# Sparse attention and ELU layer on one core: the weights queue up behind the second block's Q, block three loads on GpSimd's queue, the first batch goes in three blocks

## The chip, the core and the metric

The kernel runs on one core of one Trainium2 chip. A core has five engines that run side by side, each through its own instructions in their written order: TensorE (PE, matrix products into PSUM; PEld is its loading of the stationary operand), VectorE (DVE), ScalarE (ACT), GpSimd (POOL) and SyncE (SP, which here only issues transfers). Transfers are issued by SP, ACT or POOL and carried by 16 shared DMA engines; the profile counts those that SP and ACT issue as queues of the kind hardware_dynamic, those that POOL issues as software_dynamic. An instruction that waits holds up everything written behind it on its engine. The metric is device time in microseconds (us).

## What is computed

Four batches of eight heads, 768 positions, 64 numbers a head. Each query takes part only in its six best chunks of 32 keys, found by a bound from each chunk's smallest and largest key; then an ELU layer of two matrix products follows.

```
k_min, k_max = min, max of k over each chunk of 32          # [B, H, 24, D]
ub = sum(maximum(q * k_min, q * k_max), axis=-1)            # [B, H, S, 24], causal
top_chunks = argsort(ub)[..., -6:]
scores = where(chunk selected and causal, q @ k.T / 8, -1e9)
x = softmax(scores) @ v                                     # to [3072, 512]
h = x @ w_in                                                # [3072, 2048]
out = where(h > 0, h, exp(min(h, 0)) - 1) @ w_out           # [3072, 512]
```

## The kernel before, in words

The work is cut into eight blocks: each batch in two halves of 384 queries (BLOCKS, line 40). A block goes through these stages; heads are handled in four pairs.

- **Loads** (`load`, L347 on). K, Q and V in f32, rows of 256 bytes. The first block's are fetched head by head (L365, 96 KB each), those of all others in tiles of 128 positions (L372, 256 KB each). SP issues nearly all of them; ACT issues four K loads of the first block. POOL issues the weights, w_in in four parts (L382) and w_out in four (L387); they are cast to bf16 on the way, and POOL issues them where the order puts them: w_in behind the first block's Q casts (G_IN), w_out behind the second's (G_OUT).
- **Front** (`prep_k`, `prep_q`). PE turns each K and Q tile (L401, 3 products with the identity for a pair). DVE reduces K to chunk minima and maxima (L420, L437). ACT copies K to bf16: in the first block straight into `lhs` (L427), in others into `kb` (L432), which SP then sends to `lhs` (L435). ACT copies Q in f32 (L452); POOL casts it to bf16 in `rhs` (L461); DVE makes its positive part (L464).
- **Selection** (`select`). PE makes the bounds (L481), DVE turns them (L492), finds the sixth best (L499), compares (L503) and turns the mask (L508); SP sends it in eight transfers into rows 64 to 95 of `rhs` (L512). The same rows of `lhs` hold a constant pattern (econst), put there by DVE (L336), ACT (L338) and SP (L341), so that the score product itself adds -40000 to what is not selected.
- **Attention** (`attend`). Score products (L533), exponentials on ACT (L549, L553), the causal diagonal on DVE (L560, L567), products with V (L581; V is cast by POOL, L392), normalising on DVE (L590, L592), then the turn to the layer's layout, by PE in the first and last block (L600) and by a transposing transfer in the others (L605).
- **Layer** (`mlp`). First product (L618), exponential on ACT (L622), subtraction on POOL (L624), maximum and minimum on DVE (L626), second product (L636), copy on ACT (L640), output by SP (L643).

No loop on the chip sets the order. All steps are noted in a list, each with an engine, a supposed duration, its dependences and a due time, shifted by the table SHIFTS; `Plan.run` plays them against numbered buffers (CAPS) and the resulting order is written out, engine by engine. On the chip each engine then waits for what its next instruction needs, in that order.

Of the kernel before, what the change touches and what calls it, by code (L numbers as in the profile page):

```python
# [15 lines left out]
B = 4  # L16
# [11 lines left out]
HS = S // 2  # L28
HCH = NCH // 2
# [7 lines left out]
Q0 = TOPK * CHUNK  # L37
QLO = (Q0, HS)
QHI = (HS, S)
BLOCKS = [(b, hf) for b in range(B) for hf in range(2)]  # L40
DIRECT_K = (0, )
DIRECT_Q = ()
INIT = ("DVE", "DVE", "ACT", "ACT")
G_IN = "q0"
G_OUT = "q1"
BY_PAIR = (0, )
AFTER_MASK = 1
GATED = ()
# [67 lines left out]
class Plan:  # L116
# [38 lines left out]
    def run(self):  # L155
# [7 lines left out]
        slots = {c: [(0.0, i, None) for i in range(n)] for c, n in self.caps.items()}  # L163
        free = dict.fromkeys(("PE", "ACT", "DVE", "POOL", "SP"), 0.0)
        cand = {e: [] for e in free}
        for o in self.ops:
            if o.wait == 0:
                cand[o.eng].append(o)
        best, dirty, held = dict.fromkeys(free), set(free), set()
        hw, sw, self.order = 0.0, 0.0, []  # L170
        for o in self.ops:
            for x in o.bufs:
                x.end = 0
        while len(self.order) < len(self.ops):
            for e in dirty:
                best[e], found = None, []
                for o in cand[e]:
                    t = max(o.ready, free[e])
                    for x in o.bufs:
                        if x not in held:  # L180
                            t = max(t, min(slots[x.cls], key=lambda v: v[:2], default=(1e18, ))[0])
# [51 lines left out]
def kernel(  # L233
# [448 lines left out]
    for s in range(NPAIR):  # L682
        init_lhs(s, INIT[s])
# [73 lines left out]
```

## Time and profile before

| what | value |
|---|---|
| median of 3 runs | 326.98 us (323.62 to 327.88) |
| the profiled execution | 325.89 us, its span 324.10 us |
| PE busy | 274.39 us, 85% of the span |
| ACT, DVE, POOL busy | 193.86, 190.84, 126.26 us |
| moved by DMA over the span | 36.49 MB, 113 GB/s in the mean |
| chain that ended last | PE 57%, DMA 15%, SP's queue 11%, ACT 7% |

The span runs from the profile's first instruction to its last; 1.79 us of the execution lie outside it. A busy share over the whole span mixes a start, in which data is still coming in, with a long middle in which PE is busy almost without a break; so the stretches are read apart below. The granted clock is given as a share of full speed (1.00 is 2.4 GHz, 0.50 is 1.2 GHz).

### The profile page before, as it was taken

What the parts mean: (1) busy time and instruction counts of PE and PEld (TensorE: products, weight loads), DVE (VectorE), ACT (ScalarE), POOL (GpSimd) and SP (SyncE); (2) the same over time, 40 slices, a digit from 0 to 9 for tenths busy, and PEclk for the clock granted to TensorE, in tenths of its full rate; (3) what the DMA queues carried; (4) which work ended last, traced back from release to release, by engine and by line L of the source; (5) the groups of instructions that cost most, each with busy time, mean ns of one, the idle gap of its engine ahead of it and who ended that gap; (6) DMA issues with size and microseconds to landing.
All of it is one profiled execution on the core that took longest, in us unless ns stands there. A gap on an engine that the chain in (4) does not pass through costs nothing.

```text
span 324.1 us, 6738 instructions
## 1 busy us (share of the span) xinstructions
PE 274.4 (85%) x2300; PEld 165.1 (51%) x2328; DVE 190.8 (59%) x603; ACT 193.9 (60%) x416; POOL 126.3 (39%) x251
## 2 busy tenths in 40 slices
PE   4722870797992999799989999999999999999995
PEld 2411540464662664366646654566665645664642
DVE  7540884383871698236875986689746823651730
ACT  6512730386882674399837743798888925871731
POOL 5550193284522154235553532256415403510730
PEclk9965897699998699999999999999999999999999
DMA  8899799689967379632904692311112021002101
GB/s 168 197 203 200 161 163 199 138 166 214 205 113 170 72 166 208 134 112 55 188 16 123 130 212 81 124 33 31 38 27 72 20 63 67 2 2 91 41 32 65
DMA packets 100690, 36.49 MB, mean 113 GB/s; under 512 B 88624, under 2 KB 97584, under 8 KB 100656
## 3 DMA queue, kind: packets, MB, share of 16 engines
q1 hardware_dynamic: 94832, 31.48, 44.8%
q0 software_dynamic: 4224, 4.19, 7.9%
q10 hardware_dynamic: 1600, 0.39, 0.6%
q8 instruction: 18, 0.29, 0.4%
q14 instruction: 16, 0.13, 0.1%
HBM read 27.26 MB, written 6.29 MB: 104 GB/s over the span
## 4 chain that ended last, share of the span: by engine, by line
PE 57%; DMA 15%; SPq 11%; ACT 7%; DVE 4%; issue 4%; POOL 2%; ACTq 0%; DVEq 0%; POOLq 0%
PE psM L618 19%; PE psM L636 19%; PE psS L533 8%; DMA kld<-in_k_dram 6%; DMA rhs<-msk 5%; PE psO L581 4%; SPq L372 4%; PE psT L401 4%; ACT pt L549 3%; SPq L512 3%; SPq L365 2%; ACT e L622 2%; DMA qld<-in_q_dram 2%; POOL e L624 1%; PE psT L481 1%
## 5 line engine op out<-in xcount | busy, mean ns | idle before, releaser
L624 POOL TENSOR_SCALAR e<-e 128x384 f32<-128x384 f32 x128 | 65.9, 518 | 114.2 <-ACT e L622 105.2
L618 PE MATMUL psM<-xt,w_in_sb 128*128 128x384 bf16 x512 | 103.1, 330 | 0.4
L636 PE MATMUL psM<-w_out_sb,gT 128*128 128x512 bf16 x356 | 98.0, 381 | 2.9 <-DVE gT L626 1.6
L626 DVE SCALAR_TENSOR_TENSOR gT<-psM,e 128x384 bf16<-128x384 f32 x128 | 69.6, 553 | 40.5 <-POOL e L624 38.1
L549 ACT ACTIVATE pt<-psS 128x384 bf16<-128x384 f32 (+1 forms) x156 | 79.2, 545 | 20.5 <-PE psS L533 19.4
L622 ACT ACTIVATE e<-psM 128x384 f32<-128x384 f32 x128 | 64.0, 504 | 35.5 <-PE psM L618 34.1
L533 PE MATMUL psS<-rhs,lhs 96*128 96x384 bf16 (+2 forms) x280 | 65.2, 301 | 11.2 <-DMA rhs<-msk 10.7
L618 PEld LDWEIGHTS <-w_in_sb 128*128 128x128 bf16 x512 | 49.3, 99 | 32.8 <-issue 4.2
L636 PEld LDWEIGHTS <-gT 128*128 128x128 bf16 x384 | 36.8, 98 | 33.8 <-DVE gT L626 2.9
L461 POOL TENSOR_SCALAR rhs<-QTf 64x384 bf16<-64x384 f32 x64 | 34.4, 538 | 44.6 <-ACT QTf L452 33.3
L533 PEld LDWEIGHTS <-lhs 96*128 96x128 bf16 x288 | 27.1, 102 | 30.2 <-DMA rhs<-msk 12.4
L640 ACT ACTIVATE osb<-psM 128x512 f32<-128x512 f32 x24 | 14.1, 597 | 36.0 <-PE psM L636 35.5
L420 DVE TENSOR_REDUCE kmx<-psT 128x12 f32<-128x384 f32 x28 | 15.5, 553 | 32.9 <-PE psT L401 32.8
L401 PE MATMUL psT<-ident_f,kld 128*128 128x128 f32 x84 | 16.9, 306 | 20.6 <-DMA kld<-in_k_dram 13.2
L581 PEld LDWEIGHTS <-pt 128*128 128x128 bf16 x672 | 28.8, 99 | 8.4 <-issue 0.8
L581 PE MATMUL psO<-vext,pt 128*128 128x65 bf16 x672 | 31.9, 196 | 0.1
L392 POOL TENSOR_SCALAR vext<-vld 128x384 bf16<-128x384 f32 x32 | 15.8, 518 | 24.8 <-DMA vld<-in_v_dram 17.7
L432 ACT ACTIVATE kb<-psT 128x384 bf16<-128x384 f32 x28 | 13.9, 497 | 18.7 <-DVE kst L420 12.7
L560 DVE TENSOR_TENSOR pt<-pt,tri 128x512 bf16<-128x512 bf16 x32 | 14.4, 449 | 17.0 <-ACT pt L549 16.8
L401 PEld LDWEIGHTS psT<-ident_f,kld 128*128 128x128 f32 x84 | 10.7, 153 | 26.5 <-DMA kld<-in_k_dram 14.7
L452 ACT ACTIVATE QTf<-psT 128x384 f32<-128x384 f32 x28 | 14.1, 503 | 11.2 <-PE psT L401 11.0
L553 ACT ACTIVATE pt<-psS 128x512 bf16<-128x512 f32 x32 | 19.6, 612 | 1.5 <-PE psS L533 1.2
(59 smaller groups left out, 208.0 us busy)
## 6 DMA issues: line engine op xcount, KB each, us to landing
out_dram<-osb SPq DMA_DIRECT2D x24, 256.0 KB, 2.2
kld<-in_k_dram SPq DMA_DIRECT2D x21, 256.0 KB, 4.4
qld<-in_q_dram SPq DMA_DIRECT2D x21, 256.0 KB, 4.8
vld<-in_v_dram SPq DMA_DIRECT2D x21, 256.0 KB, 4.6
lhs<-kb SPq DMA_DIRECT2D x56, 48.0 KB, 2.2
w_in_sb<-in_moe_w_in_dram POOLq DMA_DIRECT2D x4, 512.0 KB, 10.8
w_out_sb<-in_moe_w_out_dram POOLq DMA_DIRECT2D x4, 512.0 KB, 13.3
qld<-in_q_dram SPq DMA_DIRECT2D x8, 96.0 KB, 2.8
```

The lines of the kernel that those rows point to most:

```text
L392: return op("POOL", 480, 60, lambda: nc.gpsimd.tensor_scalar(out=vexts[t % NSET][:, 3 * hf:3 * hf + 3, :, 0:D], in0=xb.get()[:, :, hs, :], ...
L401: nc.tensor.transpose(ps.get()[:, P * n:P * (n + 1)], xb.get()[:, n, hs, :].rearrange("p h d -> p (h d)"), ident_f)
L461: qcast[i, j] = pool_op(480, lambda h=h: nc.gpsimd.tensor_scalar(out=rhs[hf][0:64, h, j, :], in0=qtf.get()[64 * h:64 * h + 64], scalar1=1. ...
L533: nc.tensor.matmul(sps.get()[:, o + pc:o + pc + w], lhsT=lhs[s][0:96, hd, P * kb:P * (kb + 1)], rhs=rhs[hf][0:96, hd, j, cq:cq + w], start ...
L549: op("ACT", 390 if wtot <= 384 else 495, 130, lambda pt=pt, sps=sps, hd=hd, wtot=wtot: nc.scalar.activation(out=pt.get()[:, hd, 0:wtot], i ...
L553: op("ACT", 495, 130, lambda pt=pt, sps=sps: nc.scalar.activation(out=pt.get()[:, :, 0:256], in_=sps.get()[:, :].rearrange("p (h w) -> p h ...
L581: nc.tensor.matmul(o3.get()[:, hd, qi, :], lhsT=pt.get()[:, hd, P * qt + off:P * qt + off + P], rhs=vexts[s][:, kb, hd, :], start=(kb == 0 ...
L618: op("PE", 161, 200, lambda fc=fc, kk=kk, h_ps=h_ps: nc.tensor.matmul(h_ps.get()[:, 0:HS], lhsT=w_in_sb[:, kk, P * fc:P * (fc + 1)], rhs=x ...
L622: op("ACT", 375, 140, lambda e=e, h_ps=h_ps: nc.scalar.activation(out=e.get(), in_=h_ps.get()[:, 0:HS], func=AF.Exp), reads=[h_ps], writes ...
L624: op("POOL", 480, 110, lambda e=e: nc.gpsimd.tensor_scalar(out=e.get(), in0=e.get(), scalar1=-1.0, scalar2=1.0, op0=AOT.add, op1=AOT.mult) ...
L626: g_ops.append(op("DVE", 475, 130, lambda e=e, h_ps=h_ps, fc=fc: nc.vector.scalar_tensor_tensor(out=gT[fc // 4].get()[:, fc % 4, :], in0=h ...
L636: op("PE", 216, 200, lambda tt=tt, fc=fc, o_ps=o_ps: nc.tensor.matmul(o_ps.get(), lhsT=gT[fc // 4].get()[:, fc % 4, P * tt:P * (tt + 1)], ...
```

## The change

The first batch is cut into three blocks of 256 queries in place of two halves of 384; the other batches keep their halves, so that there are nine blocks. The planner is given another model of the transfers, and a new table SHIFTS, so the whole order is new. By name:

- SW_GATE, SW_ORDER: POOL issues no weight before a one-element copy (`spot`) of the second block's Q has run; then w_in's four parts, K and Q of the third block, two parts of w_out, V of the third block, the other two. All loads of the third block (SW_LOADS) are POOL's.
- K and Q of the first block are loaded in tiles, the second tile by ACT, behind its table load.
- DIRECT_K: K of the first two blocks goes from PSUM straight to `lhs`. QC_ACT: Q of both is cast by ACT and not by POOL. MASK_DVE: their masks are turned by DVE straight into `rhs`, one transpose a pair and head, with no transfer.
- ACT makes no econst copies; DVE makes all four of the first batch, from a smaller pattern. Early clearing of buffers moves from DVE to POOL.
- PE gets filler products of 112 columns (`junk`) where the plan leaves it idle within its first 70 us, 37 in all.

```diff
-BLOCKS = [(b, hf) for b in range(B) for hf in range(2)]
-DIRECT_K = (0, )
-INIT = ("DVE", "DVE", "ACT", "ACT")
-G_IN = "q0"
-G_OUT = "q1"
+CUTS = [(0, 256, 512, 768)] + [(0, 384, 768)] * (B - 1)
+DIRECT_K = (0,1)
+PE_T = (0, NBLK - 1)
+MASK_DVE = (0,1)
+SW_LOADS = (2,)
+SW_ORDER = ("k1", "q1", "wi0", "wi1", "v1", "wi2", "wi3", "k2", "q2", "wo0", "wo1", "v2", "wo2", "wo3")
+QC_ACT = (0,1)
+SW_GATE = ("q",1)
...
+            e = "POOL" if i in SW_LOADS else "ACT" if i == 0 and n == 1 and cls != "vld" else "SP"
...
+            if i in QC_ACT:
+                op("ACT", act_ns(w), 60, lambda h=h: nc.scalar.activation(
+                    out=rhs[RH[i]][0:64, h, j, 0:w], in_=qtf.get()[64 * h:64 * h + 64, 0:w], func=AF.Copy),
+                    reads=[qtf], writes=[r_q[RH[i]][j]])
+                continue
...
+            if i in MASK_DVE:
+                for j in range(NPAIR):
+                    op("DVE", 180 + 1.02 * nq, 50, lambda h=h, j=j, sb=sb: nc.vector.transpose(
+                        out=rhs[y][64:96, h, j, q0:w],
+                        in_=sb[32 * j:32 * j + 32, 0:nb].rearrange("p b c -> p (b c)")),
+                        reads=[r_sb], writes=[r_m[y][h][j]])
+                continue
...
+        gate_ops.append(op("POOL", 120, 60, lambda: nc.gpsimd.tensor_copy(out=spot[:, 0:1], in_=gx.get()[0:1, 0, 0, 0:1]),
+                           reads=gr, hold=[gx]))
...
+            if o.eng == "PE":
+                if 3e3 < o.start < FILL_END:
+                    for _ in range(int((o.start - pe - FILL_MIN) / FILL_NS)):
+                        nc.tensor.matmul(o_bank[:, 400:512], lhsT=junk, rhs=junk[:, 0:112], start=True, stop=True)
```

On POOL, from the first V cast on, the order before was this (L392 casts V, L461 casts Q, L382 and L387 are w_in and w_out):

```order
L392 TENSOR_SCALAR vext_80<-vld 128x6x64
L461 TENSOR_SCALAR rhs_98<-QTf 64x384 x8
L382 DMA w_in_sb<-in_moe_w_in_dram 128x4x512 x4
L392 TENSOR_SCALAR vext_81<-vld 128x6x64
L392 TENSOR_SCALAR vext_82<-vld 128x6x64
L392 TENSOR_SCALAR vext_83<-vld 128x6x64
L461 TENSOR_SCALAR rhs_99<-QTf 64x384 x2
L387 DMA w_out_sb<-in_moe_w_out_dram 128x4x512 x4
```

From the end of the first block's V casts on, it now is this (L778 is the one-element copy, L435 loads K, Q and V, L711 is the layer's subtraction):

```order
L467 TENSOR_SCALAR vext_85<-vld 128x4x64
L778 COPY spot<-qld 1x1
L451 DMA w_in_sb<-in_moe_w_in_dram 128x4x512 x4
L467 TENSOR_SCALAR vext_82<-vld 128x4x64
L467 TENSOR_SCALAR vext_83<-vld 128x4x64
L467 TENSOR_SCALAR vext_84<-vld 128x4x64
L467 TENSOR_SCALAR vext_85<-vld 128x4x64
L435 DMA kld<-in_k_dram 128x8x64 x2
L435 DMA qld<-in_q_dram 128x8x64 x2
L455 DMA w_out_sb<-in_moe_w_out_dram 128x4x512 x2
L435 DMA vld<-in_v_dram 128x8x64
L711 TENSOR_SCALAR e<-e 128x256 x4
```

The Q casts have left POOL, and K, Q and V of the third block stand between the two weights.

On SP, from the program's start, the order before was this (L372 is the second block, L512 the first block's masks):

```order
L365 DMA kld<-in_k_dram 128x3x64 x4
L365 DMA qld<-in_q_dram 128x3x64 x8
L365 DMA vld<-in_v_dram 128x3x64 x8
L372 DMA kld<-in_k_dram 128x8x64 x3
L372 DMA qld<-in_q_dram 128x8x64 x3
L512 DMA rhs_98<-msk 32x192 x8
L435 DMA lhs_88<-kb 64x384 x2
```

And this now (two tiles each of V of the first block, then K, Q and V of the second; behind the econst transfers, L413, the fourth block's K and Q in three tiles each):

```order
L435 DMA kld<-in_k_dram 128x8x64
L435 DMA qld<-in_q_dram 128x8x64
L435 DMA vld<-in_v_dram 128x8x64 x2
L435 DMA kld<-in_k_dram 128x8x64 x2
L435 DMA qld<-in_q_dram 128x8x64 x2
L435 DMA vld<-in_v_dram 128x8x64 x2
L413 DMA lhs_94<-econst 32x2x768
L413 DMA lhs_95<-econst 32x2x768
L413 DMA lhs_96<-econst 32x2x768
L413 DMA lhs_97<-econst 32x2x768
L435 DMA kld<-in_k_dram 128x8x64 x3
L435 DMA qld<-in_q_dram 128x8x64 x3
```

The masks of the first two blocks are gone from SP, and the fourth block's loads stand where they stood.

On PE, in the middle of the second block's scores (L617; `rhs_101` is that block's Q), the order now is this; L476 turns a K tile of the third block, L705 is the layer's first product:

```order
L617 LDWEIGHTS lhs_91
L617 MATMUL psS<-rhs_101,lhs_91 128x256
L617 LDWEIGHTS lhs_91
L617 MATMUL psS<-rhs_101,lhs_91 128x256
L476 MATMUL psT<-ident_f,kld 128x128 x2
L617 LDWEIGHTS lhs_91
L617 MATMUL psS<-rhs_101,lhs_91 128x256
L617 LDWEIGHTS lhs_91
L617 MATMUL psS<-rhs_101,lhs_91 128x128
L705 LDWEIGHTS w_in_sb
L705 MATMUL psM<-xt,w_in_sb 128x256
```

The third block's K, which comes on POOL's queue behind w_in, now has scores of the second block behind it on PE.

## Rows read from the trace of the kernel before

**Rows 1.** Stretches: start:end, length, busy us (count) PE PEld DVE ACT POOL, clock, DMA share, GB/s.

```profile
0.00:16.00 16.00, 8.94 (x57) 5.43 (x57) 10.60 (x40) 9.74 (x16) 8.67 (x28) 1.00 0.87 182
16.00:32.00 16.00, 3.80 (x15) 1.79 (x16) 3.78 (x15) 2.21 (x5) 5.01 (x8) 0.57 1.23 202
32.00:48.00 16.00, 13.34 (x145) 8.51 (x143) 12.68 (x56) 9.45 (x20) 7.84 (x14) 0.90 0.83 160
48.00:64.00 16.00, 5.82 (x22) 2.97 (x23) 6.41 (x15) 2.62 (x6) 5.00 (x10) 0.68 0.99 176
...
80.00:324.10 244.10, 228.21 (x1954) 137.33 (x1980) 146.36 (x454) 157.39 (x342) 89.12 (x172) 0.99 0.39 90
```

**Rows 2.** Chain that ended last: start us, length us, what (times).

```profile
21.43 9.24 DMA rhs<-msk
43.26 15.00 DMA kld<-in_k_dram
69.13 0.33 PE psT L401 x3
100.09 3.31 DMA lhs<-kb
292.77 6.69 PE psM L636 x31
299.46 10.40 PE psM L618 x64
```

**Rows 3.** Timeline of PE: start us, us, engine, line, operation [idle before, releaser].

```profile
29.61 0.61 PE L533 MATMUL psS<-rhs,lhs 96*128 96x384 bf16 x2 [8.27 <-DMA rhs<-msk]
58.30 0.48 PE L401 MATMUL psT<-ident_f,kld 128*128 128x128 f32 x1 [7.45 <-DMA kld<-in_k_dram]
80.11 0.33 PE L401 MATMUL psT<-ident_f,qld 128*128 128x128 f32 x1 [1.04 <-DMA qld<-in_q_dram]
104.04 0.90 PE L401 MATMUL psT<-ident_f,kld 128*128 128x128 f32 x3 [5.71 <-ACT kb L432]
```

**Rows 4.** Tile w_in_sb: issues (ns min/median/max, first and last start us), then landing.

```profile
L382 POOL DMA_DIRECT2D w_in_sb<-in_moe_w_in_dram x4: 747/756/956, 16.4 to 18.9; - x4
...
DMA to landing us min/median/max: 6.9/10.8/14.0
```

**Rows 5.** Tile w_out_sb: the same.

```profile
L387 POOL DMA_DIRECT2D w_out_sb<-in_moe_w_out_dram x4: 750/766/867, 40.7 to 43.1; - x4
...
DMA to landing us min/median/max: 9.4/13.3/17.3
```

**Rows 6.** DMA queues from 16 to 32 us: packets, MB, share of 16 engines.

```profile
q0 software_dynamic: 2096, 2.09, 77.9%
q1 hardware_dynamic: 4467, 1.15, 45.0%
```

**Rows 7.** Groups by line and shape: count | busy us, mean ns | idle before.

```profile
L508 DVE STREAM_TRANSPOSE msk<-selb 128x384 bf16<-128x384 bf16 x8 | 4.3, 556 | 0.0
L427 ACT ACTIVATE lhs<-psM 64x384 bf16<-64x384 f32 x8 | 3.7, 482 | 0.1
L338 ACT ACTIVATE lhs<-econst 32x1536 bf16<-32x1536 bf16 x2 | 3.0, 1480 | 0.0
L508 DVE STREAM_TRANSPOSE msk<-selb 128x192 bf16<-128x192 bf16 x8 | 2.9, 360 | 0.0
L618 PEld LDWEIGHTS <-w_in_sb 128*128 128x128 bf16 x512 | 49.3, 99 | 32.8 <-issue 4.2
```

**Rows 8.** Timeline of ACT and DVE in the first 17 us, columns as in rows 3.

```profile
3.03 1.28 ACT L303 ACT_TABLE_LOAD   x1 [3.03 <-issue]
...
16.84 0.38 DVE L508 STREAM_TRANSPOSE msk<-selb 128x192 bf16<-128x192 bf16 x1
```

More of the change, by code (lines that the diff above doesn't have):

```diff
@@ L87 @@
+VC_ACT = ()
+SW_GATE = ("q",1)
+SW_OCC = 1000
 LAG = 1
@@ L169, in run, with over @@
         best, dirty, held = dict.fromkeys(free), set(free), set()
-        hw, sw, self.order = 0.0, 0.0, []
-        for o in self.ops:
-            for x in o.bufs:
-                x.end = 0
-        while len(self.order) < len(self.ops):
+        lanes = {"POOL": [0.0] * 8, "SP": [0.0] * 8}
+        lanes["ACT"], full_rings, self.order = lanes["SP"], {}, []
+        lane_of, turn = dict(POOL="POOL", SP="SP", ACT="SP"), dict(POOL=0, SP=0)
+        def over(e):
+            return sum(r[1] / r[2] for r in rings[e]) - RING
@@ new lines, in leave, with enter @@
+        def leave(o, end):
+            for x in o.bufs:
+                x.left -= 1
+                x.end = max(x.end, end)
+                if x.left == 0:
+                    slots[x.cls].append(x.end)
+                    dirty.update(free)
+        def enter(o, time, want):
+            for s, full in succ[o]:
+                if full is want:
+                    s.wait -= 1
+                    s.ready = max(s.ready, time)
+                    if s.wait == 0:
+                        cand[s.eng].append(s)
+                        dirty.add(s.eng)
@@ L191, in run @@
+            if done is not None:
+                done.end = clock + 1200
+                lanes[done.eng][done.lane] = done.end
+                dirty.update(("SP", "ACT", "POOL"))
+                leave(done, done.end)
+                enter(done, done.end, True)
+                continue
+            if room:
+                continue
+            if o is None:
+                break
             cand[o.eng].remove(o)
@@ L527, in attend, with part @@
         seg = {}
-        nst = len(steps[hf]) + 1
+        steps = STEPS[lo, hi]
+        nst = len(steps) + 1
+        def part(kb):
+            return max(z for z in range(len(parts) - 1) if parts[z] <= P * kb)
         def scores(sps, segs, hd, o):
-            for (kb, c0, w, pc) in segs:
-                cq = c0 - HS * hf
-                nc.tensor.matmul(sps.get()[:, o + pc:o + pc + w], lhsT=lhs[s][0:96, hd, P * kb:P * (kb + 1)],
-                                 rhs=rhs[hf][0:96, hd, j, cq:cq + w], start=True, stop=True)
@@ L721 @@
             casts(i + 2)
+        if i == 0:
+            plan.tag = ("w_out", 0)
+            span(-0.2, 0.0, 0.1)
+            for x in range(4):
+                load_w_out(x)
+        mlp(i, span(i + LAG, *SP_M))
+    last = gate_ops
+    for name in SW_ORDER:
+        for o in sw.get(name, ()):
+            for d in last:
+                o.deps.setdefault(d, False)
+            last = [o]
     for o in plan.ops:
```

631 lines of the change are left out of this document (327 added, 304 removed), and 13 rows, old and new, of tables (SHIFTS, STEPS).

## The prediction

> **What bounds the kernel now.** I read the stretches first. From 80 us to the end PE is busy 228.21 of 244.10 us at a granted clock of 0.99; in the first 64 us it is busy 8.94 + 3.80 + 13.34 + 5.82 = 31.9 us, and from 16 to 32 us at a clock of 0.57 [rows 1]. So the end is bound by PE and the start by what PE waits for. The DMA share of the start is 0.83 to 1.23 in every stretch, at 182, 202, 160 and 176 GB/s, 180 in the mean [rows 1]: the transfers are nearly always busy there, and their order decides what PE can do.
>
> The chain of waits names two stretches. The first block's masks are turned by 17.22 us (16.84 + 0.38) [rows 8], but the last one of the chain takes 9.24 us to land [rows 2], beside w_in, which POOL issues from 16.4 us on [rows 4]; PE starts the first scores at 29.61, after 8.27 us of idling, and goes on with them at about 30.7. Then a K tile of the third block takes 15.00 us [rows 2] beside w_out, issued from 40.7 us on [rows 5], and the PE, which has that tile ahead of the layer's products, goes on at 58.30 [rows 3]. In the late stretch one wait stands out: 5.71 us before 104.04, for a K copy on ACT [rows 3] that had waited for `lhs` transfers, the last of them 3.31 us [rows 2].
>
> **How far PE is.** I measure progress by the columns that PE must stream ahead of a place in its order. 64 products of 384 columns take 10.40 us and 31 of 512 take 6.69 [rows 2], 0.423 ns a column both times. An f32 turn of 128 columns takes 0.33/3 = 0.11 us [rows 2], twice that price. The bounds (L481), 9,216 columns in both orders by the places compared, are left out. Counted in the order, ahead of the wait at 80.11 us [rows 3] stand 72 turns, 41 score products (11,904 columns), 78 products with V of 65, 12 bf16 turns, 64 first-layer products of 384 and 15 second-layer ones of 512: 29.2 us. Ahead of the wait at 58.30 it is 12.35 us. Between the two, PE worked off 16.9 us in 21.8 us, a pace of 0.775.
>
> **The change, part by part.**
>
> *Bytes.* In the changed order, the last quarter of w_out is the last thing that the first layer needs. By then the queues have carried 18 tiles of the first batch, six of the fourth block (SP has them ahead) and the weights: 24 x 0.262 + 4.19 MB; and 1.04 MB of small ones (four econst of 96 KB, eight `lhs` of 32, four `xt` of 64, eight masks of 16). That is 11.5 MB: 64 us at 180 GB/s, 57 us at 202 behind a start of about 3 us. I take 62. Before, the last quarter landed at the latest at 43.1 + 17.3 = 60.4 us [rows 5], beside about the same bytes. So the change brings no bandwidth; it puts other work in front of the same end.
>
> *Masks off the queue.* Eight DVE transposes of 64 and eight of 256 columns replace four turns and sixteen transfers. From 360 ns at 192 and 556 at 384 columns [rows 7] I get about 0.23 and 0.43 us each: 5.2 us in place of 1.8 (two turns at each size). DVE is busy 10.60 + 3.78 of the first 32 us [rows 1], so the 3.4 us are hidden; without that cover they would be paid in full. The wait of 8.27 us goes. What is late next is w_in: if POOL's one-element copy runs when about nine tiles are in (2.4 MB at 182 to 202 GB/s behind 3 us, some 15 us), w_in is issued about when it was (16.4 us), and its parts land between about 23 and 33 us [rows 4].
>
> *Copies on ACT.* Removed: two econst copies of 1.48 us and eight K copies of 0.48 us, 6.8 us. Added: 16 K copies and 16 Q casts of 256 columns, at 0.32 (by columns) to 0.48 us [rows 7], say 0.36: 11.5 us. ACT is busy 9.74 + 2.21 of the first 32 us [rows 1]; the 4.7 us more are hidden, though eight casts (2.9 us) stand ahead of the first exponentials. The first block's scores then run at about 15 to 19 us, still ahead of w_in. Uncovered, the casts would cost 2.9 us, or nothing if POOL, which loses them, was later than ACT. ACT's two tiles of the first block go out behind the table load, 1.28 us [rows 8]; this too ends ahead of w_in and costs nothing.
>
> *Third block on POOL's queue.* It lands behind w_in. By the second Q tile, 21 tiles and w_in and econst are through: 8.0 MB, at 190 GB/s about 42 us. PE waits for K and Q of that block in its order, with scores of the second block behind K. No row has f32 tiles of 256-byte rows on this queue; between 16 and 32 us its packets cost 0.779 x 16 x 16 / 2096 = 0.095 us of an engine, those of SP's queue 0.0258 [rows 6]. I take SP's price, since a tile's rows are those that SP moves (the weights' packets hold 1 KB, 2.09 MB / 2096); the other end is a rival below.
>
> *Narrower layer products.* 256 columns take 0.108 us, the load of a stationary operand 0.099 [rows 7]; it stays hidden. I take 0 and at most 1 us for 104 such products behind the place compared.
>
> *Sum.* Ahead of the last quarter of w_out stand 63 turns, 48 score products, 80 with V, eight bf16 turns, 88 first-layer products of 256, 24 of the second: 28.5 us, and 1.75 us of fillers, which fill idle time. That is 0.7 us less than before at 80.11. Behind the second Q tile lie 15.8 us of it: 42 + 15.8/0.775 + about 1 us of bounds is 63.4. With the landing at 62, PE is there at about 64 us. It was there at 80.1 - 0.7/0.775 = 79.2, so 15.2 us are gained: a span of 308.9, with 1.79 outside it 310.7; I say 311.0, against 325.89 of the same execution and a median of 326.98.
>
> By the Trainium skill, *DMA: Bandwidth & Descriptors*, section *Anatomy of one DMA — SWDGE (gpsimd) path*, a DMA takes 2.0 us plus its bytes at 436 GB/s. By that figure the 24 tiles and 8.4 MB of weights as read would be in by an estimated 37 us, and the start would be PE's alone. The trace disagrees so far: 182 GB/s with one queue, 202 with two [rows 1].
>
> **The rivals.**
>
> *The third block comes late.* If its Q lands at 52 us in place of 42, because the tiles of the two queues share the engines, PE stands in front of it with the second block's scores behind, and reaches the place at 74: 321 us. At 57 us nothing is gained. For it: a K tile beside w_out took 15.00 us [rows 2]. Against: the tiles now stand in one queue with the weights and not beside it.
>
> *Slower: POOL's packets cost what they cost the weights.* At 0.095 us in place of 0.0258, six tiles of 1,024 rows take 6 x 1024 x 0.069 / 16 = 26.6 us more, all ahead of the last quarter of w_out: PE is there at 91, and the time is 338 us. It is slower by over 2% from a packet price of about 0.084 us on, since the gain and 6.5 us must be lost. For it: the only price that this queue shows. Against: by the byte both queues cost about the same (0.095/997 and 0.0258/257).
>
> *The late wait goes too.* Both orders are new throughout. If PE reaches the place at 60 us, by transfers at 202 GB/s, and the 5.71 us before 104.04 do not come again, the time is 311 - 4 - 5.7, about 301 us. For it: PE was idle in 15.9 us of the late stretch, so there is something to gain; against: nothing says that the new order has no such wait of its own.
>
> *Tiles of 256 KB move at a higher rate*, as a DMA's fixed part would be paid less often. If transfers stopped binding, PE would go at its pace from about 10 us on: 10 + 27/0.775 = 45 us, a gain of 34 and 292 us. Against: 176 GB/s from 48 to 64 us, all in tiles of that size and weights [rows 1]. The figure above, of the Trainium skill's page *DMA: Bandwidth & Descriptors*, section *Anatomy of one DMA — SWDGE (gpsimd) path*, would have it this way.
>
> **Chances and range.** The forecast 0.46, the third block late 0.23, slower by packets 0.12, the late wait gone 0.15, the higher rate 0.04. The range from 300 to 325 holds the first, the second and the fourth but their edges, and leaves out the slower one and the higher rate. A measurement of this kernel can tell about 2% from no change (320.4 and 333.5 us): faster takes the forecast, the two faster rivals and a fifth of the late block, 0.70; within 2% the rest of it, 0.18; slower 0.12.
>
> **What would show it.** In the changed profile PE should wait for no mask in the first 40 us; w_in should be issued at 15 to 17 us; Q of the third block should land at about 42 us and the last quarter of w_out at 58 to 64; PE should be busy over 38 of the first 64 us. I am wrong if the third block's tiles land after 50 us, if POOL's issue of one takes several us, if the clock falls under 0.8 in a stretch from 16 to 48 us, or if the stretch behind the first batch shows more than the 15.9 us of idle PE that it had.

## The result, and the profile after

The changed kernel takes 307.81 us (median of 4 runs, 306.13 to 308.66) beside 326.88 us of the kernel before (4 runs, 323.62 to 327.88): a ratio of 0.943, with a 95% interval from 0.936 to 0.949, so 16.6 to 20.9 us are gained. The profiled execution took 306.13 us, its span 304.40. The forecast was 311.0 us, from 300 to 325.

The stretches, in the columns of [rows 1]:

```profile
0.00:16.00 16.00, 8.89 (x76) 6.63 (x77) 10.07 (x36) 9.10 (x23) 12.94 (x39) 1.00 0.96 210
16.00:32.00 16.00, 12.98 (x102) 9.37 (x108) 10.33 (x37) 11.33 (x32) 7.48 (x12) 1.00 1.18 236
32.00:48.00 16.00, 13.30 (x153) 10.20 (x138) 13.85 (x54) 11.51 (x30) 8.12 (x18) 0.89 1.16 218
48.00:64.00 16.00, 12.87 (x122) 8.31 (x121) 10.56 (x46) 6.61 (x17) 9.39 (x23) 1.00 0.39 90
80.00:304.40 224.40, 213.36 (x1844) 129.85 (x1869) 141.68 (x446) 150.48 (x326) 87.80 (x172) 1.00 0.38 97
```

PE is busy 8.89 + 12.98 + 13.30 + 12.87 = 48.0 us of the first 64, where it was 31.9 [rows 1]. Two things moved: from 16 to 32 us PE has work (12.98 us for 3.80), and the bytes come in sooner. The first 48 us moved (210 + 236 + 218) x 16 us = 10.6 MB, before (182 + 202 + 160) x 16 = 8.7 MB [rows 1]; from 48 us on the transfers are nearly idle (0.39). In the late stretch PE is idle for 11.0 us and not 15.9.

POOL's timeline shows the weights and the third block (the columns of [rows 3]):

```profile
12.19 0.18 POOL L778 COPY spot<-qld 1x1 f32<-1x1 f32 x1 [1.75 <-DMA qld<-in_q_dram]
12.31 3.19 POOL L451 DMA_DIRECT2D w_in_sb<-in_moe_w_in_dram  x4
17.00 1.84 POOL L435 DMA_DIRECT2D kld<-in_k_dram  x2
18.83 1.76 POOL L435 DMA_DIRECT2D qld<-in_q_dram  x2
36.32 0.78 POOL L455 DMA_DIRECT2D w_out_sb<-in_moe_w_out_dram  x1
```

The four tiles of K and Q take 13.5 to 13.7 us from issue to landing, so Q of the third block is there at 19.7 + 13.5 = 33.2 us. The last part of w_out takes 11.8 us and lands at 48.1.

PE's timeline has the places that answer to [rows 3]:

```profile
16.18 0.85 PE L617 MATMUL psS<-rhs,lhs 96*128 96x256 bf16 x4
36.25 0.54 PE L617 MATMUL psS<-rhs,lhs 96*128 96x256 bf16 x4 [1.26 <-DVE rhs L583]
56.09 0.40 PE L555 MATMUL psT<-QTf,kst 64*32 64x256 f32 x1 [1.91 <-ACT kb L508]
65.38 1.03 PE L724 MATMUL psM<-w_out_sb,gT 128*128 128x512 bf16 x4
```

The first scores run at 16.18 us and not at 29.61; no product in the first 64 us waits for a mask transfer. At 65.38 PE takes up the last quarter of w_out, 13.8 us ahead of the 79.2 that the prediction had for the kernel before.

### The profile page after: what moved, and what is told of

It is laid out like the page before. It is cut to its first block, busy times and chain, and to the rows that moved or that the text cites. A ratio compares the mean times of both kernels' runs of the same rounds, so it can differ in the third digit from the quotient of the medians.

```text
span 304.4 us, 7162 instructions
## 1 busy us (share of the span) xinstructions
PE 277.3 (91%) x2449; PEld 176.8 (58%) x2481; DVE 198.4 (65%) x652; ACT 203.1 (67%) x458; POOL 133.6 (44%) x279
## 3 DMA queue, kind: packets, MB, share of 16 engines
q1 hardware_dynamic: 88128, 29.61, 39.0%
## 4 chain that ended last, share of the span: by engine, by line
PE 58%; issue 10%; DMA 10%; DVE 6%; POOL 6%; SPq 4%; ACT 4%; POOLq 0%; ACTq 0%
PE psM L705 19%; PE psM L724 18%; PE psS L617 9%; PE psT L476 5%; PE o_bank L666 5%; DMA kld<-in_k_dram 4%; DMA vld<-in_v_dram 4%; SPq L435 3%; POOL e L711 3%; POOL vext L467 2%; DVE gT L713 2%; DMA xt<-on 1%; DVE rhs L583 1%; ACT pt L633 1%; DMA rhs<-msk 1%
## 5 line engine op out<-in xcount | busy, mean ns | idle before, releaser
L711 POOL TENSOR_SCALAR e<-e 128x384 f32<-128x384 f32 (+1 forms) x144 | 68.4, 481 | 98.9 <-ACT e L709 75.5
L705 PE MATMUL psM<-xt,w_in_sb 128*128 128x384 bf16 (+1 forms) x576 | 101.9, 311 | 2.3 <-DVE gT L713 1.0
L713 DVE SCALAR_TENSOR_TENSOR gT<-psM,e 128x384 bf16<-128x384 f32 (+1 forms) x144 | 72.0, 508 | 38.4 <-POOL e L711 35.1
L633 ACT ACTIVATE pt<-psS 128x384 bf16<-128x384 f32 (+1 forms) x164 | 83.8, 546 | 15.2 <-PE psS L617 13.8
L709 ACT ACTIVATE e<-psM 128x384 f32<-128x384 f32 (+1 forms) x144 | 65.6, 460 | 31.8 <-PE psM L705 27.2
L705 PEld LDWEIGHTS <-w_in_sb 128*128 128x128 bf16 x576 | 56.1, 99 | 31.3 <-issue 3.5
L617 PE MATMUL psS<-rhs,lhs 96*128 96x256 bf16 (+2 forms) x304 | 65.2, 287 | 3.8 <-DVE rhs L583 1.3
L534 POOL TENSOR_SCALAR rhs<-QTf 64x384 bf16<-64x384 f32 (+1 forms) x56 | 29.8, 533 | 39.4 <-ACT QTf L526 19.0
L617 PEld LDWEIGHTS <-lhs 96*128 96x128 bf16 x312 | 28.9, 100 | 24.7 <-issue 5.9
L666 PE MATMUL o_bank<-vext,pt 128*128 128x65 bf16 x672 | 31.7, 196 | 1.0 <-DVE on L677 0.8
L476 PE MATMUL psT<-ident_f,kld 128*128 128x128 f32 x88 | 17.3, 294 | 5.1 <-DMA kld<-in_k_dram 2.5
L467 POOL TENSOR_SCALAR vext<-vld 128x384 bf16<-128x384 f32 (+1 forms) x36 | 16.8, 494 | 11.0 <-DMA kld<-in_k_dram 5.9
L496 DVE TENSOR_REDUCE kmx<-psT 128x12 f32<-128x384 f32 (+1 forms) x32 | 16.5, 517 | 6.7 <-PE psT L476 6.6
L677 DVE TENSOR_TENSOR on<-o_bank,rcp 128x384 bf16<-128x384 f32 (+1 forms) x36 | 18.2, 507 | 3.4 <-DMA xt<-on 2.9
L644 DVE TENSOR_TENSOR pt<-pt,tri 128x512 bf16<-128x512 bf16 x36 | 15.2, 425 | 7.7 <-ACT pt L633 7.2
L537 DVE TENSOR_SCALAR Qrl<-QTf 128x192 f32<-128x192 f32 (+3 forms) x36 | 12.3, 349 | 10.6 <-ACT QTf L526 10.5
```

What stands on the lines that cost most here:

```text
L467: return op("POOL", pool_ns(hi - lo), 60, lambda: nc.gpsimd.tensor_scalar(out=vexts[s][:, lo // P:hi // P, :, 0:D], in0=xb.get()[:, 0:nt, ...
L476: nc.tensor.transpose(ps.get()[:, P * n:P * (n + 1)], xb.get()[:, n, hs, :].rearrange("p h d -> p (h d)"), ident_f)
L534: pool_op(pool_ns(w), lambda h=h: nc.gpsimd.tensor_scalar(out=rhs[RH[i]][0:64, h, j, 0:w], in0=qtf.get()[64 * h:64 * h + 64, 0:w], scalar1 ...
L617: nc.tensor.matmul(sps.get()[:, o + pc:o + pc + n], lhsT=lhs[s][0:96, hd, P * kb:P * (kb + 1)], rhs=rhs[y][0:96, hd, j, c0 - lo:c0 - lo + ...
L633: op("ACT", act_ns(wtot), 130, lambda pt=pt, sps=sps, hd=hd, wtot=wtot: nc.scalar.activation(out=pt.get()[:, hd, 0:wtot], in_=sps.get()[:, ...
L666: nc.tensor.matmul(o3.get()[:, hd, qi, :], lhsT=pt.get()[:, hd, P * qt + off:P * qt + off + P], rhs=vexts[s][:, kb, hd, :], start=(kb == 0 ...
```

## The experiments

Two groups of kernels: the changed one with one part undone or altered, and the one before with one or more parts added. In each, the other instructions keep the planned order; only what the edit names is put elsewhere or done by another engine. "Against" is the ratio's distance to the changed kernel's 0.9427, or to 1, times 327 us.

| kernel | ratio to before, 95% interval | against |
|---|---|---|
| e1, changed, masks in SP's queue | 0.980 (0.975 to 0.985) | changed: +12.3 us |
| e2, changed, w_in at once | 0.948 (0.944 to 0.952) | changed: +1.7 |
| e3, changed, third block issued by SP | 0.945 (0.940 to 0.949) | changed: +0.8 |
| e10, changed, third block behind w_out | 0.969 (0.963 to 0.975) | changed: +8.7 |
| e8, changed, loads in 64 KB pieces | 0.999 (0.995 to 1.003) | changed: +18.5 |
| e4, changed, no fillers | 0.944 (0.939 to 0.950) | changed: +0.6 |
| e5, changed, second block's Q casts on POOL | 0.945 (0.938 to 0.952) | changed: +0.6 |
| e6, before, masks by DVE | 0.980 (0.974 to 0.986) | before: -6.4 |
| e11, e6 and third block early | 0.982 (0.975 to 0.989) | before: -5.8 |
| e7, before, eight kb buffers | 0.998 (0.994 to 1.002) | before: -0.6 |
| e9, e6 and e7 together | 0.976 (0.971 to 0.982) | before: -7.8 |
| e12, e11, e7, third block's masks by DVE | 0.966 (0.959 to 0.972) | before: -11.2 |

Distances to the changed kernel are known to about 3 us (its interval and the kernel's own together), those to before to about 2.

### The masks' way: e1 and e6

In e1, DVE turns a head's four masks at once, and SP sends them:

```diff
-                    op("DVE", ..., lambda ...: nc.vector.transpose(
-                        out=rhs[y][64:96, h, j, q0:w], in_=sb[32 * j:32 * j + 32, 0:nb]...
+                        j or nc.vector.transpose(out=m[0][:, 0:nq], in_=sb[:, 0:nb]...),
+                        nc.sync.dma_start(out=rhs[y][64:96, h, j, q0:w], in_=m[0][32 * j:32 * j + 32, 0:nq])
```

> The changed kernel, but the masks of the first two blocks take the way they took before: one turn of a head's four pairs on DVE, then four transfers on SP. The order is otherwise that of the changed kernel. Theory (the wait for the masks was the first part of the loss): the first block's masks are turned at about 14 us, land beside w_in at 20 to 24 us, the first scores move from 16.2 us to 21 to 24 us, and the time rises by 4 to 7 us, to 312 to 315 us. Rival (the start is long for the bytes that it moves, whatever waits in front of them): the work behind closes the gap, 306 to 310 us. Second rival (DVE's turns are the dearer way, since PE waits for them between 35 and 41 us): faster than the changed kernel by 1 to 2 us.

It took 320.85 us. PE's timeline:

```profile
23.10 0.98 PE L617 MATMUL psS<-rhs,lhs 96*128 96x256 bf16 x4 [6.93 <-DMA rhs<-msk]
48.54 0.90 PE L617 MATMUL psS<-rhs,lhs 96*128 96x256 bf16 x4 [5.92 <-DMA rhs<-msk]
54.03 0.93 PE L617 MATMUL psS<-rhs,lhs 96*128 96x256 bf16 x4 [2.21 <-DMA rhs<-msk]
```

The first scores slip to 23.10, as the theory had it, but the second block's masks stop PE too: SP sends them from 43.74 us on in turns with the fourth block's Q tiles, the last pair from 49.46 on. The loss of 12.3 us is twice what was expected. Both rivals fall. The other way round, e6 gives the kernel before DVE's turns:

```diff
+ENG0 = ("SP", "ACT"); MASK_DVE = (0, 1)
-            op("DVE", ..., lambda ...: nc.vector.transpose(out=msk.get()[:, 0:nq], ...
+            op("DVE", ..., lambda ...: [nc.vector.transpose(out=rhs[hf][64:96, h, j, q0:HS], in_=sb[32 * j:32 * j + 32, 0:nb]...) for j in range(NPAIR)] if i in MASK_DVE else ...
```

> The kernel before in its own order, with one part of the change: the masks of its first two blocks are turned by DVE straight into their place (16 turns of 32 partitions in place of 4 turns and 16 transfers of SP). Theory (the masks' way through the queue is the largest part): the wait of 8.27 us before 29.61 us goes, and so do the 11.7 us that SP needed to issue the first eight mask transfers, so that all behind them on SP, the third block's K above all (issued at 40.3 us before), goes out 8 to 11 us earlier; the time falls by 8 to 13 us, to 314 to 319 us. Rival (PE is only sooner in front of the third block's K, which w_out keeps late): 321 to 326 us.

It took 321.05 us, at the near edge of the rival's range and not in the theory's. No product waits for a mask in the first 80 us; but PE's timeline then has this:

```profile
51.64 0.47 PE L401 MATMUL psT<-ident_f,kld 128*128 128x128 f32 x1 [11.54 <-DMA kld<-in_k_dram]
```

The wait for the third block's K, 7.45 us in [rows 3], has grown to 11.54. As the rival had it, PE is sooner in front of a tile that comes little sooner: w_out went out earlier too (33.1 us), and SP issued K's last tile only at 48.3 us. So the masks are the largest part that was undone by itself, and worth 6.4 us or 12.3 depending on what stands behind them.

### The third block's place: e3, e10, e11

e3 issues the same six tiles on SP, at the place of the order where POOL had them:

```diff
-            def go(n=n, q=dict(SP=nc.sync, ACT=nc.scalar, POOL=nc.gpsimd)[e]):
+            def go(n=n, q=dict(SP=nc.sync, ACT=nc.scalar, POOL=nc.sync)[e]):
```

> The changed kernel, but the six tiles of the third block are issued by SP, where the planned order puts them, and not by POOL. Theory (it is the place of the block behind w_in that counts, and SP's queue runs beside POOL's): K and Q of the third block go out at 12 to 14 us and share the engines with w_in, which lands 5 to 8 us later than its 21.3 to 29.9 us; PE needs the first quarter of w_in at 28.3 us, and the place where the last quarter of w_out is needed moves by 0 to 4 us: 307 to 312 us. Rival A (one queue is as good as the other, both ends are hidden): 306 to 309 us. Rival B (tiles beside weights are slow, as the tile of 15 us was before): K or Q of the third block lands after 40 us and the time rises to 315 us or more.

309.45 us: no difference that can be told. SP issued the second Q tile only at 21.7 us; K had landed by 34.9 and Q by 39.3 us, later than in the changed kernel but still ahead of PE's turns of that Q at 43.64. e10 leaves the tiles on POOL, but K and Q behind the last part of w_out:

```diff
+        k2 = sw["k2"] + sw["q2"]; rest = [o for o in plan.order if o not in k2]; c = rest.index(sw["wo3"][-1]) + 1; order = rest[:c] + k2 + rest[c:]
```

> The changed kernel, but K and Q of the third block are issued on GpSimd's queue behind the last part of w_out (issued at 36.3 us) and not behind w_in (17 to 19.7 us). Theory (the place of this block among the weights is the second part of the gain): K lands at 43 to 48 and Q at 46 to 52 us in place of 30.7 to 33.2, PE, which has the turns of K at 36.7 us, waits 7 to 11 us, and the time is 315 to 320 us. Rival (the first layer behind it in PE's order has slack, and the w_out that now comes earlier gives it back): 308 to 312 us.

317.58 us, within the theory's range. K went out at 37.22 us, and PE's timeline shows the wait:

```profile
48.19 0.48 PE L476 MATMUL psT<-ident_f,kld 128*128 128x128 f32 x1 [11.21 <-DMA kld<-in_k_dram]
```

So the place ahead of w_out is worth 8.7 us of the changed kernel, and the issuing engine nothing. Then e11 gave the kernel before (with e6's masks) an early third block, on SP:

```diff
-        for o in plan.order:
-            o.fn()
+        for o in rest[:a] + k2 + rest[a:z] + q2 + rest[z:]: o.fn()
```

Here a is the place behind the second block's Q tiles, z the one ahead of the econst transfers.

> The kernel before with the masks of its first two blocks turned by DVE, and with the third block's K tiles issued by SP right behind the second block's Q, the third block's Q tiles ahead of the econst transfers. In that kernel without the second edit PE had waited 11.54 us for a K tile of the third block, issued at 38.7 to 48.3 us beside w_out (33.1 us). Theory (the gain is made of two places in the order of transfers, masks and third block): K goes out at about 18 to 21 us and lands by 35 us, the 13 us of waits for K go but for 2 to 5 us that the weights lose to it, and the time falls from 321 to 309 to 314 us. Rival (K beside w_in only delays w_in and the second block's lhs transfers, and PE waits for those): 317 us or more.

319.76 us: nothing gained over e6, and the rival was right. SP's and PE's timelines say why:

```profile
17.74 13.08 SPq L372 DMA_DIRECT2D kld<-in_k_dram  x3
30.92 5.33 SPq L435 DMA_DIRECT2D lhs<-kb  x4
```

```profile
37.65 0.90 PE L401 MATMUL psT<-ident_f,qld 128*128 128x128 f32 x3 [8.29 <-ACT kb L432]
54.75 5.23 PE L618 MATMUL psM<-xt,w_in_sb 128*128 128x384 bf16 x17 [6.39 <-DVE gT L626]
```

While w_in runs, SP needs 13.08 us to issue three tiles, and the second block's lhs transfers, which stand behind them, go out at 30.92 us and not at 21.40 as in e6. The K copies then find no free kb buffer, and PE waits 8.29 us for one. The changed kernel has no such transfers there, since K of both first blocks goes straight to lhs; but that this part (DIRECT_K) is what lets the third block be early is not shown: it was not undone by itself, and e12 below, whose eight kb buffers take the 8.29 us away, has run no more products on PE by 80 us than e11 (415 and 419 in the trace).

### The weights' gate: e2

```diff
+        w4 = [o for x in range(4) for o in sw[f"wi{x}"]]; rest = [o for o in plan.order if o not in w4 + gate_ops]; c = next(n for n, o in enumerate(rest) if o.key[0] == ("cast", 0)); order = rest[:c] + w4 + rest[c:]
```

> The changed kernel without the one-element copy: w_in's four parts are issued ahead of the first block's V casts, at about 5 to 8 us in place of 12.3 to 15.5 us. All else stands in the same order. Theory (the order of transfers decides): 4.2 MB at 210 to 236 GB/s are 18 to 20 us of the engines; the loads of the first two blocks share them, so that Q of the second block lands at 18 to 22 us in place of 12, the second block's turns and first scores slip by 3 to 6 us, and the time is 311 to 315 us. Rival (all these bytes are needed by the first layer's end anyway, so that their order is indifferent): 306 to 309 us.

310.12 us: 1.7 us with an interval that reaches 0. The first scores did not slip (the turns of K ahead of them run at 15.01 us, for 15.70). What slipped is V of the second block, whose casts stand on POOL ahead of the third block's loads and the layer's subtractions. POOL's timeline:

```profile
8.63 3.18 POOL L451 DMA_DIRECT2D w_in_sb<-in_moe_w_in_dram  x4
29.40 1.65 POOL L467 TENSOR_SCALAR vext<-vld 128x256 bf16<-128x256 f32 x4 [16.02 <-DMA vld<-in_v_dram]
```

PE waits 6.3 us once, before 37.96 us, for the DVE step that needs those subtractions, and regains most of that. Waiting for the second block's Q, the change's first-named part, is worth 0 to 4 us.

### The size of a load: e8

This goes further than undoing a part: the kernel before had pieces of 96 KB, and those in its first block alone.

```diff
-                q.dma_start(out=xb.get()[:, n, :, :], ...
+                for c in range(0, H, 2 if i < 3 else H): q.dma_start(out=xb.get()[:, n, c:c + (2 if i < 3 else H), :], ...
```

> The changed kernel with each tile of the first three blocks' K, Q and V loaded in four transfers of 64 KB (two heads each) in place of one of 256 KB, with the same rows of 256 bytes. The start moved 210 and 236 GB/s where before it moved 182 and 202. Theory (small transfers lower the rate or are issued too slowly: before, the first block came in 96 KB pieces): the first 32 us move 180 to 205 GB/s, the first scores come 2 to 4 us later and the time is 311 to 316 us. Rival (the rate is that of the 256-byte rows, and the size of a transfer doesn't matter; SP's issues are hidden): 308 to 310 us at an unchanged rate.

325.83 us: all of the gain is lost. The rate of the first 16 us, in 40 slices of 0.4 us; first the changed kernel, then e8:

```profile
GB/s 0 0 0 0 13 123 114 219 289 287 287 287 289 289 290 286 290 286 289 280 269 285 208 248 239 222 259 266 232 275 190 214 268 199 213 247 127 104 188 223
```

```profile
GB/s 0 0 0 0 13 200 168 224 188 137 149 231 146 152 149 231 207 175 225 214 187 207 213 191 151 133 76 118 149 138 149 113 122 126 127 111 145 148 131 123
```

SP's timeline in e8:

```profile
9.41 4.05 SPq L435 DMA_DIRECT2D kld<-in_k_dram  x8
13.51 4.06 SPq L435 DMA_DIRECT2D qld<-in_q_dram  x8
```

An issue takes 4.05 / 8 = 0.51 us, about as long as that of a whole tile (0.45 and 0.57 us for SP's first two in the changed kernel). With 64 KB (65.5 kB) in each, SP alone can start 129 GB/s, and e8's slices from 10 us on show 76 to 149, with the 16 engines only 3 to 6 tenths busy (a digit a slice, 9 for 90% or more):

```profile
DMA  0000087986696669979989986535666555546655
```

With tiles of 262 kB the same issues could start about 500 GB/s; the engines set the pace, at 286 to 290. In the kernel before, 20 of the first block's 24 pieces of 98 kB went through SP at the same 0.51 to 0.52 us, 190 GB/s by that arithmetic, beside the 182 of [rows 1]. Its own slices of the first 16 us agree:

```profile
DMA  0000089999999999999897778888778975599999
GB/s 0 0 0 0 6 192 268 247 274 262 222 233 224 222 214 211 192 183 207 179 225 156 179 170 190 184 184 194 176 176 197 215 173 133 129 217 277 271 287 222
```

From 8 to 12 us, while SP alone issues pieces, they show 156 to 225 with the engines 7 to 9 tenths busy; from 14.4 to 15.6 us, behind the issues of the second block's tiles, 271 to 287. So the size of the first loads makes the rate of the start; no run gave the kernel before larger ones. The 18.5 us are not the rate's alone: V of the second block came so late that POOL's casts of it ended at 35.3 us (17.05 in the changed kernel), and 16 issues of K and Q on POOL then took another 11.6 us, for 3.6. PE waited 17.38 us behind that. The granted clock was lower as well: 0.80, 0.50, 0.61 and 0.71 in the four stretches of the first 64 us, for 1.00, 1.00, 0.89 and 1.00. The three were not told apart.

### Fillers and casts: e4 and e5

```diff
-FILL_END = 70e3
+FILL_END = 0
```

> The changed kernel without its 37 filler products on PE, in the same order otherwise. Theory (they stand in time that PE waits, and PE's progress at the start is set by what it waits for): 306 to 309 us. Rival (they keep PE busy where it waits and so hold the granted clock at 1.00 in the first 32 us, where it was 0.57 before): the clock of the stretch from 16 to 32 us falls under 0.8 and the time rises by 3 to 8 us, to 311 to 316 us.

308.56 us, and a granted clock of 1.00 from 16 to 32 us without any filler, with PE busy for 13.16 us of them: the fillers can go. e5 runs the second block's eight Q casts on POOL:

```diff
-                op("ACT", ..., lambda h=h: nc.scalar.activation(out=rhs[RH[i]][0:64, h, j, 0:w], ...)
+                op("ACT", ..., lambda h=h: nc.scalar.activation(...) if i == 0 else nc.gpsimd.tensor_scalar(out=rhs[RH[i]][0:64, h, j, 0:w], ...)
```

> The changed kernel, but the second block's eight Q casts run on GpSimd, as before, and not on ScalarE; they stand behind the first two parts of w_out in its order. Theory (the casts are hidden on either engine): 307 to 310 us. Rival (GpSimd is held up by the issues of w_out, so that Q comes late and the second block's scores at 36.2 us wait): 311 to 316 us. Second rival (ScalarE's 3 us less let PE's waits for it between 22 and 57 us shrink): 304 to 306.5 us.

308.43 us: the second block's casts are hidden on either engine. The first block's were not moved.

### The late wait: e7, e9, e12

```diff
-        return Buf(cls, lambda: p.tile(shape, dtype, name=cls, tag=cls, bufs=CAPS[cls]))
+        return Buf(cls, lambda: p.tile(shape, dtype, name=cls, tag=cls, bufs=8 if cls == "kb" else CAPS[cls]))
```

> The kernel before, instruction for instruction, but with eight buffers for the K copies (kb) in place of three, so that the copy of 103.50 us need not wait until a transfer to lhs has freed one. Theory (the late wait of 5.71 us stands on its own and delays all behind it): it goes, and the time falls by 4 to 6 us, to 321 to 323 us. Rival (the transfers behind are late all the same, and PE meets the next one): 325 to 328 us.

327.55 us: nothing. The wait of 5.71 us went as foretold, but PE's timeline has two others in its place:

```profile
107.62 0.75 PE L581 MATMUL psO<-vext,pt 128*128 128x65 bf16 x12 [4.27 <-DVE on L592]
112.17 1.76 PE L618 MATMUL psM<-xt,w_in_sb 128*128 128x384 bf16 x5 [2.15 <-DMA xt<-on]
```

Both hang on the turning transfers to xt, which stand in SP's order behind eight mask transfers (92.07, 5.78 us), three V tiles and four lhs transfers, and go out at 103.68. The buffers were the place where PE met the late queue, not the reason.

e9 puts this edit and that of e6 together.

> The kernel before with both: masks of the first two blocks turned by DVE, and eight buffers for the K copies. Theory (these two waits are what the change takes away, the rest of it is worth little): the gains add up to 13 to 18 us, and the time is 309 to 314 us, near the changed kernel's 308 to 309. Rival (the change needs its other parts, the place of the third block's loads and the three blocks): 316 us or more.

319.54 us: 1.4 us under e6, within the intervals, so the buffers bring as little as in e7; the 13 to 18 us did not come, and the rival was right.

e12 takes those eight mask transfers off the queue, too; beside this line it has e7's eight buffers and all of e11:

```diff
-ENG0 = ("SP", "ACT"); MASK_DVE = (0, 1)
+ENG0 = ("SP", "ACT"); MASK_DVE = (0, 1, 2)
```

> The kernel of the run above, further with eight buffers for the K copies and with the third block's masks, too, turned by DVE, so that SP's queue loses the eight mask transfers of 5.58 us that stood before the late wait. Theory (the late wait is made by SP's queue: with more buffers alone PE waited 4.27 and 2.15 us for turning transfers behind the same eight): the late waits shrink from 6 to under 2 us, and the time is 3 to 6 us under the run above. Rival (DVE's dearer turns or the next transfers in SP's queue take it): within 2 us of the run above.

314.86 us, by the ratios 5.5 us under e11, and the intervals don't touch. No wait of PE behind 80 us is longer than 2.04 us. In the stretches of e11 and of e12 the wait, and what the clock did behind it, can be seen:

```profile
96.00:104.00 8.00, 6.20 (x44) 4.46 (x46) 3.41 (x10) 4.62 (x9) 1.94 (x4) 0.57 0.42 103
```

```profile
96.00:104.00 8.00, 6.90 (x66) 4.49 (x64) 5.99 (x18) 6.43 (x14) 2.04 (x4) 1.00 0.41 102
```

In e11 the 5.46 us of waiting end at 97.59, and the stretch behind them runs at 0.57 of the clock (44 products in 6.20 us); in e12, at 1.00, 66 products take 6.90. So with those eight transfers off SP's queue the late wait goes. The eight buffers alone do not take it away, neither in e7 nor in e9, whose PE waits 4.40 us before 99.19:

```profile
96.00:104.00 8.00, 2.76 (x20) 1.64 (x20) 2.79 (x8) 1.47 (x3) 1.72 (x4) 0.63 0.36 87
```

Whether the masks' edit would do it without the buffers was not tried.

e12 still lacks 7.5 us of the changed kernel's gain. What it does not have is the first block in tiles, K of the second block straight to lhs, and three blocks in the first batch; which of these carries the rest stays open. No kernel of these beats the changed one; e3, e4 and e5 equal it, so the fillers, the engine of the second block's casts and the issuer of the third block are free choices.

## Why the prediction was right, and where not

- **Start bound by the order of the transfers, end by PE.** Right: the masks' place (12.3 us) and the third block's place (8.7 us) decide, and 13.8 of 19.7 us of span are gained ahead of the place compared. But not the order alone: with smaller loads in the same order (e8) all of it is lost.
- **Bytes: "the change brings no bandwidth".** This step failed. The count of bytes was good (11.5 MB were foretold ahead of the last quarter of w_out; the first 48 us moved 10.6, the first 64 us 12.1), but they were in at 48.1 us and not at 62. I took the rate of a start that SP's issues had held down as the rate of the transfers. That accounts for (210 - 182) x 16 us = 0.4 of the 1.9 MB that the first 48 us moved more. From 16 to 32 us another 0.5 MB came with the third block's tiles on POOL's queue; e3, which has them on SP's, moved 199 GB/s there, no more than the kernel before, and took the same time in all. The last 0.9 MB came from 32 to 48 us, where the kernel before had its engines at a share of 0.83 and issued K of the third block only from 40.3 us on; no run took that apart. The rival with 256 KB tiles, at 0.04, had the direction right for the first 16 us, with SP's 0.51 us an issue as the fixed part, and the price wrong: with the bytes in early, PE was held by its own work and by DVE, so its 292 us did not come. The figure from the Trainium skill, *DMA: Bandwidth & Descriptors*, section *Anatomy of one DMA — SWDGE (gpsimd) path*, made an estimated 37 us of it; the trace, at 48.1, lies between the two, and its best slices reach 346 GB/s.
- **Masks by DVE.** The sizes were right, and the cover half so:

```profile
L583 DVE STREAM_TRANSPOSE rhs<-selb 32x256 bf16<-32x256 bf16 x8 | 3.5, 436 | 0.2
L583 DVE STREAM_TRANSPOSE rhs<-selb 32x64 bf16<-32x64 bf16 x8 | 1.9, 236 | 0.2
```

  These are groups by shape of DVE in the first 66 us: 0.44 and 0.24 us, 5.4 in all, for 0.43, 0.23 and 5.2. For the first block's PE shows no wait, though some lie in the chain that ended last, from 16.86 to 18.39 us; the second block's lie in it from 35.77 to 40.5 us, and PE waits 1.26 us for the first of them.
- **w_in issued at 15 to 17 us.** It was 12.31, as Q of the second block landed by 12.2: the same error in the rate.
- **ACT.** The casts took 0.415 us each for 0.36. The second block's are hidden, by e5. The first block's are not, though the prediction put them at nothing: four of them stand on ACT ahead of the second block's K copies, in that chain as well, and PE waits for the copy behind them:

```profile
13.02 1.70 ACT L530 ACTIVATE rhs<-QTf 64x256 bf16<-64x256 f32 x4
15.70 0.69 PE L476 MATMUL psT<-ident_f,kld 128*128 128x128 f32 x2 [1.63 <-ACT lhs L503]
```

  What that is worth in the end was not tried. The first scores at 16.18 lie in the 15 to 19 foretold.
- **Third block.** Foretold at 42 us for Q, landed at 33.2. The rival of the dear packets fell, since its six tiles did not become 6 x 1024 packets on that queue (below). POOL's issue took 0.9 us each.
- **Sum.** PE at the place at 64 us foretold, 65.38 measured: a gain of 13.8 us for 15.2. But not by the way foretold. Q landed 9 us early; PE came to its turns only at 43.77 us, held by DVE's masks and its own order, and from there took 21.6 us for the 15.8 + 1 us of work, a pace of 0.78. The pace was well measured; that PE began on it at 43.77, where I had 42 for a landing, is chance: in e3, with Q there at 39.3 us, PE came to it at 43.64.
- **The late wait.** 5.9 of the gained us lie behind that place; the forecast had none there, the rival of the late wait (0.15) 5.7. In the changed kernel the longest waits of PE behind 64 us are these (us in total, times, longest):

```profile
PE psT L476 <- DMA kld<-in_k_dram: 0.9, 2, 0.6
PE o_bank L666 <- DVE on L677: 0.8, 2, 0.6
PE psT L476 <- DVE ubT L566: 0.7, 1, 0.7
```

  With 15.2 and 5.7 the sum would have been 305.0; the measured 306.13 of that execution lies between it and the forecast.

## What to carry to other kernels

A short start that is "bound by transfers" may be bound by their issue: divide the bytes of one transfer by the time of one issue before taking the measured rate for the engines' own, and load in pieces large enough that this quotient lies above it. Where a wait is taken away, look for what stands next in that engine's order and whether it comes sooner as well; here the masks were worth 6.4 us where the next tile stayed late and 12.3 where it did not. A wait for a buffer can be only the place where a late queue is met: look at what stands in that queue as well, since here further buffers alone (e7, e9) moved the wait and didn't shorten it.

## What the runs showed of the hardware

**Packets by issuer.** The queues of the changed kernel, then of e3, over the whole span (packets, MB, share of 16 engines):

```profile
q1 hardware_dynamic: 88128, 29.61, 39.0%
q0 software_dynamic: 4704, 5.77, 10.0%
```

```profile
q1 hardware_dynamic: 94368, 31.18, 41.4%
q0 software_dynamic: 4224, 4.19, 8.4%
```

The same six tiles (1.58 MB of 256-byte rows) make 480 packets of 3.3 kB when POOL issues them and 6,240 of 252 bytes when SP does. From 16 to 32 us the two kernels moved 236 and 199 GB/s.

**SP's queue beside POOL's.** From 23 to 32 us of the changed kernel:

```profile
q0 software_dynamic: 1406, 2.12, 105.9%
q1 hardware_dynamic: 662, 0.17, 11.5%
```

SP's queue got 0.17 of 2.30 MB, though the fourth block's K tiles stood in it from 23 us on. SP's own issues are held up as well:

```profile
L435 SPq DMA_DIRECT2D qld<-in_q_dram x3: 3467/6145/8372, 30.1 to 44.7; - x3
```

One issue took 3.5 to 8.4 us (ns min/median/max), in place of 0.51. By the Trainium skill, *DMA: Bandwidth & Descriptors*, section *Queues, rings and completion order*, an engine takes turns between its queues by whole packets; the trace agrees in part: the queue with the larger packets (1.5 kB in the mean, for 0.26) got most of the bytes, but it also sent 1,406 packets for 662, where one packet in turn would give equal numbers.

**The clock behind a wait.** Behind the late wait the granted clock was lower in each kernel that had it: 0.57 and 0.63 in the stretches of e11 and e9 above, and in the kernel before, whose 5.71 us end at 104.04, this:

```profile
104.00:112.00 8.00, 7.65 (x52) 5.29 (x54) 4.90 (x15) 5.42 (x11) 1.14 (x3) 0.61 0.35 74
```

But a wait does not always bring it. In e7, whose PE has the same order of instructions, it waits 8.13 us for the first masks, and the clock stays at 1.00 from 16 to 32 us, where the kernel before had 0.57 [rows 1]:

```profile
16.00:32.00 16.00, 4.20 (x15) 1.98 (x16) 3.92 (x16) 2.31 (x5) 5.15 (x8) 1.00 1.23 202
```

So a wait can cost more than its own length; when it does, and how much more, was not measured.
